# K^T V of two more batches in one float32 pass instead of three float16 passes, with a new issue order

## The chip, the cores and the metric

The kernel runs on one core of a Trainium2 chip. The metric is the device time of one execution in microseconds (us). The kernel before was timed at 987.38 us, the median of three runs (986.22 to 987.43 us).

## The reference, cut to what matters

Three layers are chained: a linear attention with exponential features, a gated feed-forward layer and an ELU feed-forward layer. All inputs are float32.

```python
# attention: B=4 batches, H=8 heads, S=576 tokens, D=64, m=128 features
phi(x) = exp(x @ omega.T - |x|^2/2 - max) / sqrt(m)     # per token and head: 128 features
q_p, k_p = phi(q / 64**.25), phi(k / 64**.25)
kv  = einsum('bhsm,bhsd->bhmd', k_p, v)                 # K^T V, one 128 x 64 matrix per batch and head
z   = sum(k_p, axis=2)
out = einsum('bhsm,bhmd->bhsd', q_p, kv) / (einsum('bhsm,bhm->bhs', q_p, z) + 1e-6)
# x: 2304 tokens x 512
xn  = rmsnorm(x) * rms_g
x   = (silu(xn @ w_gate) * (xn @ w_val)) @ w_out        # d_ff 1536
y   = elu(x @ w_in) @ w_out2                            # d_ff 2048
```

## The kernel before

Large products are made in float16 pairs: a float32 operand is split into a high part (rounded to float16) and a low part (the rest), and three products (high x high, high x low, low x high) are summed in PSUM. These products, with 256 columns each, make up the two feed-forward layers; the kernel calls them the spine. Nine blocks of 256 tokens go through them; the last layer uses a Strassen form with seven products.

The attention is cut into jobs. A *k job* takes one tile of 128 tokens of K (the fifth tile of a batch has 64), makes the features of 8 heads in `phi`, and adds this tile's part of K^T V to two PSUM banks, `acc`. A batch has five k jobs, so four batches have 20. A *q job* makes the features of 128 query tokens, multiplies them by the finished K^T V, divides, normalizes, and transposes the result for the spine. The k jobs of batches 0 and 1 run in the first 130 us, while weights are still loaded and split. Those of batches 2 and 3 lie between spine products; their tiles of K^T V run on TensorE at 293 to 326 us (batch 2) and 418 to 443 us (batch 3).

There are two ways to form K^T V, chosen by the batch number against `KV32` (2 in this kernel), in `k_job`, `values`, `phi` and `turned`:

- Batches below `KV32`: the features stay float32 (`phi` is called with `pair=False` and returns `d`). V is loaded as float32 with a column of ones for z (65 columns per head) from the input `v1`. Each head takes one float32 matmul, with V as the 65 weight columns and the features as 128 moving columns. The sum is K^T V transposed, 65 x 512 in each bank. After the last tile, `turned` splits it into a high and a low part (ScalarE and VectorE), turns each head back with a small float16 matmul against the identity (16 per batch: two parts of eight heads), and copies the results to the pair `kv_r` that the q jobs read.
- Other batches: V and the features are both split into float16 pairs. Per tile that is a copy to float16 and a subtraction over 1024 columns for the features (`halves` in `phi`) and a scaled copy and a subtraction over 512 columns for V (`values`). Each head takes three float16 matmuls with the features as 128 weight columns and 65, 64 and 65 moving columns. The last tile's sum is already in the right shape and is split once.

```python
e = phi(load, n, key, b >= KV32)
...
if b < KV32:
    pe.matmul(out=acc[h // 4][0:65, ...], lhsT=V32[:n, t, h], rhs=e[:n, h * P:(h + 1) * P], ...)
...
    pe.matmul(out=o, lhsT=kh, rhs=V[:n, t, h, 0:65], ...)
    pe.matmul(out=o[:, 0:64], lhsT=kh, rhs=V[:n, t, h, 65:129], ...)
    pe.matmul(out=o, lhsT=kl, rhs=V[:n, t, h, 0:65], ...)
```

The order of all work is set by a planner (`Plan`). Every operation is first recorded; then `deadlines` gives each a due time counted back from the spine, `order` plays the program through with estimated costs and takes on each engine the ready operation that is due first, and `play` issues the instructions in that order. All instructions therefore carry the line of `play` (L530) in the profile. The numbers that steer it (`BIAS` per job, `PRICE` for the choice between engines that can do the same step, `LOOK`, `INFL`, `LEAD`, `STRETCH`, `AHEAD`, `PELEAD`, and `BLIM` for PSUM banks held by the attention) stand at the head of the file. Names in the profile: RX, RW, RA, RM, RC, RS, RI and RO are areas of SBUF that are used for different things in turn, `ps` is any of the eight PSUM banks.

Of the kernel before, what the change touches and what calls it, by code (L numbers as in the profile page):

```python
# [22 lines left out]
NACT, SPLIT = '12111011102010110100001022111212110111', '00000000000000001111111111111111111111'  # L23
SPINE = [(0, 0), (0, 1), (0, 2), (1, 0), (1, 1), (0, 3), (0, 4), (1, 2), (0, 5), (1, 3), (1, 4), (1, 5)]
TPE = 1
KV32 = 2
HALF = 2
AHEAD, BLIM = 1540580.623, 6
QPE = 3
FINE = 9  # L30
BIAS = [1, -22, 0, -12, 8, 10, 1, -7, -6, 14, 26, 7, 0, 2, -36, -40, 59, 0, 26, -23, 0, -36, 41, -65, -115, 60, 0, -2, -73, -72, 0, -47, -43, -15, 226, -101, -257, -27, 0, 11, -9, -26, 15, 25, 55, 0, 3, 53, -60, 1, -17, 1, 102, 7, 7, -1, 0, 28, -17, 3, 56, 56]
LOOK, WEIGH = 0.076, 80
PRICE = [2.561, 1.313, 0.814, 2.417, 0.6, 0.917]
PELEAD = 127543.557
INFL, LEAD = 1.668, 51.224
STRETCH = (11.923, 880.565, 0.234)
NBLK = NT // NB
EXPM = 0x7F800000
SGN = -(1 << 31)
# [100 lines left out]
class Plan:  # L140
# [164 lines left out]
    def deadlines(self):  # L305
        at = 0.0
        for op in self.ops:
            op.due = 1e9
            if op.spine:
                op.due = at  # L310
                at += op.cost * (STRETCH[0] if at < STRETCH[1] else STRETCH[2])
        for op in reversed(self.ops):
# [3 lines left out]
    def order(self, limit=None):  # L316
        for op in self.ops:
            op.due -= BIAS[op.job] * (not op.spine)
        left = [len(op.deps) for op in self.ops]
# [74 lines left out]

        early, late = [dict(zip(("DVE", "ACT", "POOL"), p)) for p in (PRICE[:3], PRICE[3:])]
        idle = {kind: [x for x in xs if not x.closed] for kind, xs in self.slots.items()}
# [8 lines left out]
        while True:  # L405
# [37 lines left out]
            now, e = t, e = best  # L443
            op = min((op for op in queue[e] if op.now <= t + LOOK), key=lambda op: (op.due - (PELEAD if e == "PE" and not op.spine else 0.0), op.n))
            op.at = op.now
# [94 lines left out]
def fused(ctx: ExitStack, tc: tile.TileContext, qT, kT, kTt, qn, kn, v, v1, omT, eye, g, wg, wv, wo, w1, w2, out):  # L540
# [433 lines left out]
    def values(b):  # L974

        vraw = []
        for t in range(5):
            n = P if t < 4 else 64
            if b < KV32:
                sp.dma_start(out=V32[:n, t].rearrange("p h d -> p (h d)"), in_=v1[b * S + t * P:b * S + t * P + n])  # L980
            else:
# [3 lines left out]
                sp.dma_start(out=vraw[t], in_=v[b * S + t * P:b * S + t * P + n])  # L985
        if b < KV32:
            W = V32.rearrange("p t h d -> p (t h) d")[:, :, 0:64]
# [5 lines left out]
        vec.tensor_scalar(out=ivs[:, b:b + 1], in0=iv, scalar1=32768.0, scalar2=None, op0=ALU.mult)  # L993
        if b < KV32:
            vec.memset(sv, 2.0 ** -8)
# [30 lines left out]
    def k_job(b, t, key):  # L1026
# [9 lines left out]

        e = phi(load, n, key, b >= KV32)
        if t == 0:
            values(b)
        first, last = t == 0, t == 4  # L1040
        if first:
            acc[:] = [bank.next(), bank.next()]
        if b < KV32:
            with plan.group():
# [400 lines left out]
```

## Time and profile before

| | us |
|---|---|
| median of three runs | 987.38 |
| the profiled execution's own time | 987.1 |
| span from its first to its last instruction | 985.3 |
| TensorE (PE) busy | 919.1 |
| VectorE (DVE) busy | 662.1 |
| GpSimd (POOL) busy | 621.6 |
| ScalarE (ACT) busy | 541.7 |

The span is what the trace covers; 1.8 us lie around it. Busy time is the union of an engine's instructions. The clock that TensorE was granted was 0.972 of full speed on average; it is below full speed mainly in the first 130 us.

### The profile page before, as it was taken

How to read it: one execution, taken by the hardware profiler on the slowest of the kernel's cores; microseconds unless marked ns; L12 is line 12 of the kernel's file. 1: busy time of each engine (PE TensorE's matmuls, PEld its weight loads, DVE VectorE, ACT ScalarE, POOL GpSimd, SP SyncE). 2: the span in 40 equal slices, each digit the busy share in tenths (PEclk: the TensorE clock that was granted, in tenths of full speed). 3: DMA queues.
4: the chain of work that ended last, by engine and by line, in shares of the span. 5: the costliest groups of instructions: out<-in, count | busy, mean ns of one | idle time of the engine just before them, and what ended most of it. 6: DMA issues, size and time to landing. Idle time of an engine off the chain costs nothing. (4 is left out here: it accounts for less than half of the span.)

```text
span 985.3 us, 22369 instructions
## 1 busy us (share of the span) xinstructions
PE 919.1 (93%) x8904; PEld 808.2 (82%) x8904; DVE 662.1 (67%) x1618; ACT 541.7 (55%) x1014; POOL 621.6 (63%) x676
## 2 busy tenths in 40 slices
PE   6486789999989999999999999999999999999998
PEld 5386678788878878888887778888888888888887
DVE  6876899856678775768985886377626475365642
ACT  6886554625556756664643456777535564354630
POOL 2669766856969688788664568999515264152630
PEclk9587899999999999999999999999999999999999
DMA  9954554123331252124765433100000000000001
GB/s 260 231 155 142 161 173 169 28 55 87 76 87 55 66 108 71 33 77 140 187 220 130 137 120 108 65 1 7 12 23 12 12 12 17 18 17 12 12 12 43
DMA packets 82567, 82.57 MB, mean 84 GB/s; under 512 B 52896, under 2 KB 57888, under 8 KB 82464
## 3 DMA queue, kind: packets, MB, share of 16 engines
q1 hardware_dynamic: 82464, 81.16, 29.6%
q8 instruction: 69, 1.13, 0.5%
q14 instruction: 34, 0.28, 0.1%
HBM read 59.90 MB, written 8.91 MB: 70 GB/s over the span
## 5 line engine op out<-in xcount | busy, mean ns | idle before, releaser
L530 PEld LDWEIGHTS <-RW 128*128 128x128 f16 x4864 | 457.7, 99 | 79.3 <-issue 16.4
L530 PE MATMUL ps<-RM,RW 128*128 128x256 f16 (+1 forms) x3240 | 369.1, 272 | 5.7 <-POOL RW L530 2.4
L530 PEld LDWEIGHTS <-RA 128*128 128x128 f16 (+2 forms) x2984 | 257.6, 98 | 33.5 <-issue 3.6
L530 PE MATMUL ps<-RX,RA 128*128 128x256 f16 x1728 | 196.3, 273 | 1.3 <-DVE RM L530 1.2
L530 POOL TENSOR_TENSOR RA<-RA 64x512 f16<-64x512 f32 (+4 forms) x108 | 144.9, 1343 | 40.0 <-ACT RA L530 14.5
L530 ACT ACTIVATE RM<-ps,RC 128x512 f32<-128x512 f32 (+1 forms) x135 | 90.0, 669 | 103.1 <-PE ps L530 66.4
L530 ACT ACTIVATE RM<-RM 128x512 f32<-128x512 f32 (+3 forms) x166 | 98.1, 594 | 39.2 <-DVE RM L530 34.3
L530 DVE SCALAR_TENSOR_TENSOR ps<-ps,RM 128x512 f32<-128x512 f32 x72 | 50.2, 697 | 91.7 <-POOL RM L530 91.6
L530 POOL TENSOR_SCALAR RM<-RM,RC 128x512 f32<-128x512 f32 x72 | 55.3, 768 | 84.9 <-ACT RM L530 84.4
L530 POOL TENSOR_TENSOR RM<-RM 128x512 f16<-128x512 f32 (+1 forms) x97 | 95.7, 994 | 12.5 <-ACT RM L530 6.6
L530 DVE TENSOR_REDUCE RS<-ps 128x4 f32<-128x512 f32 (+5 forms) x146 | 75.0, 536 | 36.4 <-PE ps L530 36.0
L530 PE MATMUL ps<-RX,RW 128*128 128x256 f16 x864 | 98.5, 273 | 0.2 <-DVE RA L530 0.2
L530 ACT ACTIVATE RA<-RA 128x512 f32<-128x512 f32 (+3 forms) x88 | 66.7, 769 | 56.3 <-DVE RA L530 19.9
L530 DVE SCALAR_TENSOR_TENSOR RM<-RM,ps 128x512 f32<-128x512 f32 x108 | 73.0, 680 | 36.2 <-ACT RM L530 25.0
L530 POOL TENSOR_TENSOR RW<-RM,RW 128x256 f16<-128x256 f32 (+1 forms) x67 | 48.1, 727 | 39.3 <-ACT RW L530 24.8
L530 PE MATMUL ps<-RW 128*128 128x256 f16 x600 | 71.7, 273 | 0.9 <-DVE RM L530 0.9
L530 ACT ACTIVATE RA<-RA,RS 64x512 f16<-64x512 f32 (+3 forms) x71 | 53.0, 758 | 29.9 <-POOL RS L530 19.5
L530 PE MATMUL ps<-RW,RA 128*128 128x256 f16 (+2 forms) x560 | 67.0, 273 | 1.2 <-DVE RM L530 1.2
L530 POOL TENSOR_SCALAR RA<-RA,RS 64x512 f32<-64x512 f32 (+3 forms) x67 | 48.3, 721 | 24.9 <-ACT RA L530 21.4
L530 DVE TENSOR_TENSOR RM<-ps,RM 128x256 f32<-128x256 f32 x108 | 45.0, 420 | 10.5 <-ACT RM L530 6.2
L530 POOL TENSOR_SCALAR RX<-RX 128x512 int32<-128x512 uint32 x36 | 26.7, 742 | 40.1 <-DMA RX<-wg 13.9
L530 DVE SCALAR_TENSOR_TENSOR RM<-ps,RC,RM 128x256 f32<-128x256 f32 x54 | 25.1, 478 | 39.6 <-PE ps L530 35.7
(143 smaller groups left out, 1194.7 us busy)
## 6 DMA issues: line engine op xcount, KB each, us to landing
RA<-w SPq DMA_DIRECT2D x32, 512.0 KB, 4.0
RX<-wg SPq DMA_DIRECT2D x12, 512.0 KB, 5.2
RX<-wv SPq DMA_DIRECT2D x12, 512.0 KB, 6.0
RX<-wo SPq DMA_DIRECT2D x12, 512.0 KB, 4.9
out<-RM SPq DMA_DIRECT2D x36, 128.0 KB, 1.7
f<-RA SPq DMA_DIRECT2D x8, 512.0 KB, 3.0
RA<-f SPq DMA_DIRECT2D x8, 512.0 KB, 3.3
RA<-qn SPq DMA_DIRECT2D x11, 256.0 KB, 3.0
```

The lines of the kernel that those rows point to most:

```text
L530: getattr(real, fn)(*[fix(x) for x in a], **{i: fix(x) for i, x in k.items()})
```

## The change

`KV32` goes from 2 to 4, so all four batches take the float32 way. For the ten k jobs of batches 2 and 3 (eight tiles of 128 tokens, two of 64) the pairs of V and of the features are no longer made, and the 24 float16 matmuls per tile are replaced by 8 float32 matmuls. The host passes all of V with its column of ones. `turned` now runs for batches 2 and 3 too. The planner's numbers are other ones, and so the order on every engine is another. The table of `BIAS` has 62 numbers, of which most differ; its rows are left out here.

```diff
-KV32 = 2
+KV32 = 4
 HALF = 2
-AHEAD, BLIM = 1540580.623, 6
+AHEAD, BLIM = 3299112.986, 7
...
-LOOK, WEIGH = 0.076, 80
-PRICE = [2.561, 1.313, 0.814, 2.417, 0.6, 0.917]
-PELEAD = 127543.557
-INFL, LEAD = 1.668, 51.224
-STRETCH = (11.923, 880.565, 0.234)
+LOOK, WEIGH = 0.188, 80
+PRICE = [2.546, 1.318, 0.828, 2.103, 0.651, 0.872]
+PELEAD = 553133.854
+INFL, LEAD = 1.882, 50.766
+STRETCH = (9.752, 1069.521, 0.403)
```

Two places on TensorE's queue show what moved. The first is a tile of batch 2 in the middle of the program, among spine products (`ps<-RM,RW 128x256`). Before, LDWEIGHTS are the features and the rows with 64 columns are the products with the low part of V:

```order
L530 MATMUL ps_65<-RM,RW 128x256
L530 LDWEIGHTS RA
L530 MATMUL ps_62<-RA 128x65
L530 LDWEIGHTS RA
L530 MATMUL ps_62<-RA 128x64
L530 LDWEIGHTS RA
L530 MATMUL ps_62<-RA 128x65
```

Now three tiles of batch 2 follow each other there, each as two rows of four float32 matmuls (their weight loads are part of the row); RX and RA hold features and V:

```order
L530 LDWEIGHTS RW
L530 MATMUL ps_66<-RM,RW 128x256
L530 MATMUL ps_63<-RA 65x128 x4
L530 MATMUL ps_64<-RA 65x128 x4
L530 MATMUL ps_63<-RX,RA 65x128 x4
L530 MATMUL ps_64<-RX,RA 65x128 x4
L530 MATMUL ps_63<-RA 65x128 x4
L530 MATMUL ps_64<-RA 65x128 x4
L530 LDWEIGHTS RA
L530 MATMUL ps_68<-RA 128x65
```

In place of 24 short matmuls with their own weight loads a tile has 8 float32 ones, and the tiles are taken together.

The second place is the start of the spine on TensorE. Before, the first spine product (`ps_65<-RM,RW 128x128`) follows a q job's last product and three small matmuls that spread a maximum (RI, RS):

```order
L530 MATMUL ps_61<-RA,RW 128x65
L530 LDWEIGHTS RS
L530 MATMUL ps_62<-RI,RS 1x128
L530 LDWEIGHTS RI
L530 MATMUL ps_62<-RS,RI 128x1
L530 LDWEIGHTS RS
L530 MATMUL ps_64<-RI,RS 1x128
L530 LDWEIGHTS RW
L530 MATMUL ps_65<-RM,RW 128x128
```

Now two float32 tiles of batch 1 and the projection of another k job (`<-RC,RA 128x128`, eight rows) stand ahead of the first spine product, which comes 12 rows further on:

```order
L530 MATMUL ps_64<-RI,RM 128x128
L530 MATMUL ps_68<-RA 65x128 x4
L530 MATMUL ps_62<-RA 65x128 x4
L530 MATMUL ps_67<-RC,RA 128x128
L530 MATMUL ps_61<-RC,RA 128x128
```

Before, these two tiles stood behind the first 24 rows of the spine.

## Rows read from the trace of the kernel before

**Rows 1.** The page: busy time, share of the span and instructions of TensorE
```profile
PE 919.1 (93%) x8904; PEld 808.2 (82%) x8904; DVE 662.1 (67%) x1618; ACT 541.7 (55%) x1014; POOL 621.6 (63%) x676
```

**Rows 2.** Windows: length, busy time of five engines, TensorE's clock, DMA share
```profile
0.00:150.00 150.00, 106.47 (x976) 95.14 (x977) 117.36 (x303) 101.00 (x180) 98.31 (x112) 0.84 0.67 187
150.00:600.00 450.00, 435.11 (x4492) 377.59 (x4492) 337.65 (x816) 242.68 (x405) 323.91 (x306) 0.99 0.39 104
600.00:985.00 385.00, 377.48 (x3439) 335.49 (x3437) 207.06 (x500) 198.06 (x430) 199.43 (x259) 1.00 0.06 20
...
200.00:300.00 100.00, 96.61 (x1000) 83.40 (x998) 64.17 (x177) 48.61 (x76) 70.62 (x72) 0.98 0.34 78
300.00:400.00 100.00, 98.04 (x1055) 85.69 (x1053) 71.82 (x184) 62.01 (x113) 83.08 (x83) 0.98 0.32 76
```

**Rows 3.** Waits of TensorE from 200 to 500 us: total, times, longest
```profile
PE ps L530 <- DVE RS L530: 2.4, 3, 1.1
PE ps L530 <- DMA RM<-RA: 2.0, 1, 2.0
PE ps L530 <- POOL RA L530: 0.9, 1, 0.9
```

**Rows 4.** Waits of TensorE from 500 to 640 us
```profile
PE ps L530 <- DVE RA L530: 3.7, 4, 2.2
PE ps L530 <- DVE RS L530: 3.3, 4, 1.3
```

**Rows 5.** Waits of TensorE from 150 to 200 us, the longest in total
```profile
PE ps L530 <- POOL RW L530: 2.4, 3, 1.2
```

**Rows 6.** Timeline of TensorE (start, length): two tiles of batch 2, what follows
```profile
292.94 0.90 PE L530 MATMUL ps<-RA 128*128 128x65 f16 x24
293.68 0.90 PE L530 MATMUL ps<-RA,RX 128*128 128x65 f16 x24
294.42 1.06 PE L530 MATMUL ps<-RO,RA 128*128 128x128 f16 x16
```

**Rows 7.** Groups by form on TensorE: rows with 64 columns, float16 k tiles alone
```profile
L530 PE MATMUL ps<-RA 128*128 128x64 f16 x40 | 4.0, 195 | 0.0
L530 PE MATMUL ps<-RA,RX 128*128 128x64 f16 x24 | 2.5, 195 | 0.0
L530 PE MATMUL ps<-RA,RX 64*128 64x64 f16 x16 | 1.7, 192 | 0.0
```

**Rows 8.** Timeline of TensorE: four float32 tiles of batch 0 in a row
```profile
58.02 7.29 PE L530 MATMUL ps<-RW,RA 128*65 128x128 f32 x64
65.25 0.22 PE L530 MATMUL ps<-RI,RS 128*2 128x128 f16 x1
```

**Rows 9.** Timeline of TensorE: a quarter of turned for batch 1
```profile
132.00 0.29 PE L530 MATMUL ps<-RI,RA 65*128 65x65 f16 x4
132.12 1.48 PE L530 MATMUL ps<-RM,RW 128*128 128x256 f16 x12
```

**Rows 10.** Groups by form on ACT, POOL, DVE: pairs of features, steps of turned
```profile
L530 ACT ACTIVATE RA<-RA 128x1024 f16<-128x1024 f32 x13 | 13.8, 1060 | 2.1 <-POOL RA L530 1.3
L530 POOL TENSOR_TENSOR RA<-RA 128x1024 f16<-128x1024 f32 x18 | 38.4, 2132 | 19.8 <-ACT RA L530 14.5 <-DVE RS L530 3.1 <-DVE RC L530 1.6
L530 ACT ACTIVATE RA<-ps,RC 65x512 f16<-65x512 f32 x2 | 1.2, 676 | 0.0
L530 DVE SCALAR_TENSOR_TENSOR RA<-ps,RC,RA 65x512 f16<-65x512 f32 x2 | 1.4, 730 | 0.0
```

**Rows 11.** Waits of TensorE from 0 to 150 us, the two longest in total
```profile
PE ps L530 <- DVE RS L530: 16.0, 7, 4.5
PE ps L530 <- ACT RW L530: 10.9, 7, 5.1
```

**Rows 12.** Groups by form of weight loads: float16 features, float32 V
```profile
L530 PEld LDWEIGHTS <-RA 128*128 128x128 f16 x2888 | 254.0, 98 | 32.6 <-issue 2.8 <-POOL RA L530 2.2 <-DVE RM L530 1.0
L530 PEld LDWEIGHTS ps<-RW,RA 128*65 128x65 f32 x64 | 7.0, 138 | 0.1
```

More of the change, by code (lines that the diff above doesn't have):

```diff
@@ L25 @@
 TPE = 1
-KV32 = 2
+KV32 = 4
 HALF = 2
-AHEAD, BLIM = 1540580.623, 6
+AHEAD, BLIM = 3299112.986, 7
 QPE = 3
 FINE = 9
-BIAS = [1, -22, 0, -12, 8, 10, 1, -7, -6, 14, 26, 7, 0, 2, -36, -40, 59, 0, 26, -23, 0, -36, 41, -65, -115, 60, 0, -2, -73, -72, 0, -47, -43, -15, 226, -101, -257, -27, 0, 11, -9, -26, 15, 25, 55, 0, 3, 53, -60, 1, -17, 1, 102, 7, 7, -1, 0, 28, -17, 3, 56, 56]
-LOOK, WEIGH = 0.076, 80
-PRICE = [2.561, 1.313, 0.814, 2.417, 0.6, 0.917]
-PELEAD = 127543.557
-INFL, LEAD = 1.668, 51.224
-STRETCH = (11.923, 880.565, 0.234)
+BIAS = [1, -23, -4, -4, 8, 10, 6, -6, -8, 20, 28, 4, 6, -1, -28, -78, 104, 0, -43, -37, -5, -37, 38, -145, -110, -3, -4, -9, -29, -44, -7, 0, -33, 48, 123, -93, -395, -46, 0, 13, -13, -40, -1, 224, 51, -14, -1, 134, -12, 74, -14, 12, 281, 20, 0, -3, 10, 47, -17, 3, 1, 0]
+LOOK, WEIGH = 0.188, 80
[3 more added lines that the diff above has]
+STRETCH = (9.752, 1069.521, 0.403)
 NBLK = NT // NB
```

## The prediction

> **What bounds the kernel now.** I read the busy shares first: TensorE is busy for 919.1 of 985.3 us, and no other engine is above 67% [rows 1]. A busy share is an average, so the windows come next. From 150 us on TensorE is nearly without gaps: it is idle for 450.0 - 435.1 = 14.9 us between 150 and 600 us and for 385.0 - 377.5 = 7.5 us after that, but for 150.0 - 106.5 = 43.5 us in the first 150 us, where VectorE, ScalarE and GpSimd prepare weights and features [rows 2]. So there are two regimes. Work added to TensorE at the start may be hidden in its waits, while work added after 150 us moves the end one for one unless a wait disappears for it. The third view is the waits of TensorE by stage. Between 200 and 500 us they come to 5.3 us in three groups, 2.4 us of it on VectorE, 2.0 us on a transposing DMA and only 0.9 us on GpSimd [rows 3]. Between 500 and 640 us it waits 7.0 us, all on VectorE [rows 4].
>
> The edit belongs to the second regime. The K^T V tiles of batches 2 and 3 run at 293 to 443 us. The order after keeps them there: three tiles of batch 2 follow each other among spine products, as the first pair of pieces shows.
>
> **The change part by part.**
>
> *Float16 tiles removed.* The products with 64 columns exist in these tiles alone, and there are 40 + 24 + 16 = 80 of them, eight per tile: ten tiles [rows 7]. Two tiles that follow each other start 0.74 us apart, and the next group starts 0.74 us after that [rows 6]; I count starts because the last matmul's end overlaps what follows. Ten tiles take 7.4 us. That the two tiles with 64 tokens cost the same is taken over from the full ones: the moving columns are the same.
>
> *Float32 tiles added.* The same step exists for batch 0: four tiles in a row take 65.25 - 58.02 = 7.23 us, or 1.81 us each [rows 8]. They have 8 heads with 128 moving columns, exactly what the new tiles have. Ten take 18.1 us. Net: 18.1 - 7.4 = +10.7 us on TensorE.
>
> *turned added.* A quarter of it delays the spine by 132.12 - 132.00 = 0.12 us [rows 9]; four quarters and two batches are +1.0 us. It also brings a chain that was not there: ScalarE (676 ns) and VectorE (730 ns) split each of two banks, TensorE turns, and two engines copy out [rows 10], before the first q job of that batch can multiply. TensorE has spine products to run meanwhile: in the new order four quarters of batch 2 stand apart from each other with spine rows between them. I cost the latency at nothing. Without that cover it would be two banks in a row, 2 x (0.68 + 0.73) = 2.8 us per batch, 5.6 us in all.
>
> *Pairs no longer made.* Each of ten tiles loses a copy to float16 (1.06 us on ScalarE where it goes there) and a subtraction (2.13 us on GpSimd) [rows 10], so up to 10.6 us of ScalarE and 21.3 us of GpSimd go, and more for V. These engines are busy for 242.7 and 323.9 of 450 us in that stage [rows 2], so they do not set the end; the saving is worth only those waits of TensorE that it removes. Lowest is nothing. Highest is all of TensorE's idle time from 150 to 600 us, 14.9 us, plus the time that a lowered clock cost: the granted clock is 0.98 in each of the windows 200 to 300 and 300 to 400 us [rows 2], which is 0.02 x 200 = 4.0 us. I take a value near the low end, 0.9 us, the wait on GpSimd that stands in the stage itself [rows 3]. The waits on VectorE I leave where they are, because VectorE is given turned's steps and loses little, and those after 500 us come from splitting the weights of the last layer, which the change does not touch.
>
> *New order.* At the start two float32 tiles of batch 1 and a projection now stand ahead of the first spine product, as the second pair of pieces shows. The projection is 8 float32 matmuls of 128 columns as well, so three times 1.81 us, 5.4 us of TensorE time, moved forward. TensorE waits there anyway, 16.0 us for VectorE's small reductions and 10.9 us for ScalarE [rows 11], so I cost it at nothing; uncovered it is +5.4 us. It could also help, as the tiles are then out of the way later, where TensorE is already dense: they take 3.6 us there. Between -3.6 and +5.4 us I take 0, the value that the wide idle time of the start is nearest to.
>
> *Sum.* The profiled execution took 987.1 us, of which the span is 985.3 us. 987.1 + 10.7 + 1.0 - 0.9 = 997.9 us. The median of the runs lies 0.3 us above the profiled execution, so 998.2; I forecast 998 us.
>
> [...] Loading 128 float16 columns of weights takes 98 ns and there are 24 loads in a tile, and yet the tile passes in 0.74 us [rows 6, 12]: the loads overlap each other or the matmuls. [...]
>
> **The rivals.**
>
> *First, the other side: TensorE's waits go.* Place: between spine products from 150 to 640 us. The jobs of batches 2 and 3 lose their pairs, features and weights are ready earlier, and TensorE finds its operands when it comes to them. Price: up to 14.9 + 4.0 = 18.9 us back against 11.7 us added, 987.1 + 11.7 - 18.9 = 979.9 us at the extreme. It decides from 13.7 us recovered (11.7 us plus 2 us of resolution), about three quarters of all that is there; its time is some 983 us. For it: GpSimd is busy for 72% of that stage and TensorE waits on it there and, for 2.4 us, between 150 and 200 us [rows 5]. Against it: most of the waits are on VectorE and on a DMA [rows 3, 4], and a new order brings waits of its own.
>
> *Second: the start becomes longer.* The three groups moved ahead of the spine are not hidden, because what they need from ScalarE and VectorE is on the same path as the first spine products: +5.4 us, 1003.6 us with the median's 0.3 us. For it: TensorE's waits at the start are on these two engines [rows 11]. Against it: 43.5 us of idle time [rows 2].
>
> *Third: weight loads set the pace of small matmuls.* Then a float16 tile costs 24 x 98 ns = 2.35 us and a float32 one 16 x 138 ns = 2.21 us [rows 12]; ten tiles and turned are -1.4 + 1.0 = -0.4 us, 987 us. Against it stands the direct spacing of 0.74 us [rows 6].
>
> That the change does not do what it says is ruled out by the order: the rows with 64 columns are gone and ten pairs of float32 rows have come.
>
> **How the numbers follow.** The forecast has a chance of 0.76; its own range is 993 to 1004 us (the lower bound with 5 us of waits recovered, the upper with turned's latency open). The longer start has 0.08, the waits that go 0.13, and weight loads that set the pace 0.03. A difference of 0.2%, 2 us, is about what a measurement of this kernel can tell from no change. Slower by more than that are the longer start and the forecast but for a tail of 0.05 in which recovered waits eat the addition nearly up: 0.08 + 0.71 = 0.79. Within it: 0.05 + 0.03 = 0.08. Faster: 0.13. The range that holds the time 8 times in 10 is 985 to 1005 us: it reaches past the third rival at 987 and past the second at 1003.6, and leaves out most of the first.
>
> **What the profile of the changed kernel would show.** Right: float32 groups of 65 weight columns with twice the count, 1.8 us per tile at 290 to 450 us; TensorE's busy time up by 11 to 12 us, to about 931 us; its idle time about as before, some 66 us; GpSimd and ScalarE less busy. The spine's stages from 640 us on keep their length and start some 10 us later. Wrong: TensorE idle for less than 53 us in all would mean that the waits paid for the work. A first spine product more than 3 us later than before, with the end later by as much beyond the 11 us, would be the second rival. Float32 tiles that take 2.8 us would mean a lowered clock where they run, 10 us more. Less than 0.5 us between the old and the new tile would mean that I took the cost of a tile wrongly.

## The result and the profile after

The changed kernel took 992.81 us, the median of 5 runs (992.01 to 996.73), beside 987.38 us of the kernel before (986.22 to 987.55): a ratio of 1.0072, 95% interval 1.0047 to 1.0097. In a later set of runs (a1 below) it took 993.89 us, the median of 12 runs, beside 990.1 us: 1.0036 (1.0017 to 1.0056). It is slower by about 4 to 5.5 us. 998 us was forecast, 10.6 us more than before: the sign was right, the size two to three times too large. The profiled execution took 996.55 us, 3.7 us above its own median, with a span of 994.8 us.

The busy line answers to [rows 1]:

```profile
PE 930.3 (94%) x8856; PEld 818.6 (82%) x8856; DVE 657.7 (66%) x1636; ACT 524.3 (53%) x989; POOL 568.1 (57%) x635
```

TensorE has 11.2 us more work and GpSimd 53.5 us less. TensorE's idle time is 994.8 - 930.3 = 64.5 us, 1.7 us less than before. In a1's profile (span 992.1 us, TensorE busy 930.6 us) it is 61.5 us.

The windows (length, busy time of PE, PEld, DVE, ACT, POOL, clock, DMA share, GB/s) answer to [rows 2]:

```profile
0.00:150.00 150.00, 105.57 (x970) 94.94 (x971) 119.87 (x305) 99.72 (x179) 97.40 (x110) 0.86 0.70 199
150.00:600.00 450.00, 439.05 (x4381) 381.80 (x4381) 323.77 (x808) 222.38 (x379) 266.86 (x263) 0.99 0.37 99
```

The middle stage became denser, but this one row hides that two things of opposite sign happened in it. Finer windows of the kernel before show where it was idle:

```profile
150.00:200.00 50.00, 46.62 (x460) 40.46 (x460) 45.04 (x83) 25.93 (x39) 37.62 (x29) 1.00 0.29 88
200.00:500.00 300.00, 294.48 (x3183) 257.14 (x3180) 215.55 (x543) 171.24 (x299) 227.69 (x225) 0.99 0.36 91
500.00:640.00 140.00, 133.03 (x1208) 114.09 (x1206) 94.08 (x228) 73.66 (x115) 98.43 (x90) 1.00 0.42 126
```

The same windows of the changed kernel:

```profile
150.00:200.00 50.00, 44.51 (x416) 37.63 (x416) 39.36 (x88) 27.14 (x41) 33.20 (x27) 0.93 0.25 69
200.00:500.00 300.00, 299.09 (x3091) 263.62 (x3089) 206.85 (x530) 152.31 (x271) 191.74 (x193) 1.00 0.35 88
500.00:640.00 140.00, 135.18 (x1239) 115.51 (x1237) 96.92 (x243) 71.07 (x113) 79.57 (x79) 1.00 0.40 127
```

Length minus TensorE's busy time gives its idle time by stage, in us (the last line is the total less the others):

| stage | before | after | after, a1 |
|---|---|---|---|
| 0 to 150 | 43.5 | 44.4 | 42.7 |
| 150 to 200 | 3.4 | 5.5 | 5.5 |
| 200 to 500 | 5.5 | 0.9 | 0.5 |
| 500 to 640 | 7.0 | 4.8 | 4.8 |
| from 640 | 6.8 | 8.9 | 8.0 |
| total | 66.2 | 64.5 | 61.5 |

From 200 to 640 us the waits fell by 6.8 us; from 150 to 200 us they grew by 2.1 us and the clock fell from 1.00 to 0.93 there.

The waits of TensorE (who it waited for, us in total, times, longest) from 200 to 500 us answer to [rows 3]; its three groups are gone (a fourth of 0.2 us, not shown there, makes the 5.5 us of the table), and this one has come:

```profile
PE ps L530 <- DMA RX<-RA: 0.7, 1, 0.7
```

From 500 to 640 us, answering to [rows 4]:

```profile
PE ps L530 <- DVE RA L530: 2.1, 4, 0.9
PE ps L530 <- DVE RS L530: 1.7, 4, 0.6
PE ps L530 <- DMA RX<-RA: 0.6, 1, 0.6
```

From 150 to 200 us, answering to [rows 5]; the waits on GpSimd are gone, and one of 4.0 us on VectorE has come:

```profile
PE ps L530 <- DVE RW L530: 4.0, 1, 4.0
PE ps L530 <- DVE RC L530: 1.5, 1, 1.5
```

The timeline of TensorE (start, length) shows the first new tiles of batch 2 and a quarter of turned, answering to [rows 6, 8, 9]:

```profile
295.92 1.91 PE L530 MATMUL ps<-RA 128*65 128x128 f32 x16
297.67 1.91 PE L530 MATMUL ps<-RX,RA 128*65 128x128 f32 x16
299.41 2.65 PE L530 MATMUL ps<-RA 128*65 128x128 f32 x40
...
328.40 0.29 PE L530 MATMUL ps<-RI,RX 65*128 65x65 f16 x4
328.52 1.48 PE L530 MATMUL ps<-RM,RW 128*128 128x256 f16 x12
```

The first new tile takes 297.67 - 295.92 = 1.75 us where 1.81 us were predicted, and this quarter of turned 0.12 us as predicted. From start to start the ten new tiles take 1.75 to 1.89 us, 18.2 us in all; the ten old ones took 0.74 to 0.84 us, 7.8 us in all; the eight quarters take 0.12 to 0.22 us, 1.3 us in all.

Counting the 7032 spine products of 256 columns by their order in the trace, the start of the n-th (us) shows when time is lost and regained:

| n | before | after | a1 |
|---|---|---|---|
| 0 | 104.5 | 102.7 | 102.0 |
| 200 | 154.7 | 155.2 | 153.8 |
| 300 | 165.6 | 168.6 | 167.2 |
| 400 | 178.0 | 186.8 | 185.3 |
| 2000 | 397.3 | 398.5 | 397.0 |
| 2300 | 437.2 | 447.2 | 445.8 |
| 4000 | 645.8 | 653.3 | 650.6 |
| last | 981.8 | 990.9 | 988.3 |

The spine starts 1.8 us earlier and loses that and 0.5 us more by n = 200. It loses 8.3 us from there to n = 400, between 155 and 187 us, long before the first new tile. It regains 7.6 us by n = 2000 although batch 2's tiles lie in that stretch, and loses 8.8 us again where all five tiles of batch 3 are.

**What happens at 160 to 175 us.** TensorE in the changed kernel (the bracket is the idle time ahead of a row and who ended it):

```profile
164.63 5.41 PE L530 MATMUL ps<-RM,RW 128*128 128x256 f16 x48
174.07 0.27 PE L530 MATMUL ps<-RI,RC 128*6 128x128 f16 x1 [4.03 <-DVE RW L530]
174.28 6.76 PE L530 MATMUL ps<-RM,RW 128*128 128x256 f16 x36
```

VectorE meanwhile:

```profile
161.42 1.21 DVE L530 TENSOR_REDUCE RS<-RA 128x1 f32<-128x1024 f32 x1
...
163.14 0.67 DVE L530 TENSOR_REDUCE RS<-RA 64x1 f32<-64x512 f32 x1
...
168.55 0.47 DVE L530 TENSOR_SCALAR RX<-RX 128x512 uint16<-128x512 uint16 x1
172.25 0.43 DVE L530 TENSOR_SCALAR RW<-RX 128x512 int32<-128x512 int32 x1 [3.23 <-DMA RX<-wo]
```

And SyncE's queue, which issues the loads, in the changed kernel and then in the kernel before:

```profile
152.63 13.24 SPq L530 DMA_DIRECT2D RX<-wo  x4
```

```profile
146.46 15.16 SPq L530 DMA_DIRECT2D RX<-wo  x7
```

The first two rows of VectorE are two of the three pieces of the maximum of V for batch 2, which the new order places here (the first piece stands at 106.63 us; before, five shorter pieces stood between 149.61 and 195.27 us). Then VectorE stands for 3.23 us at an instruction that needs the last part of w_out. That load is the last of four issued between 152.63 and 165.87 us; before, the last was issued by 161.62 us and VectorE did not wait for it. The queue waits for VectorE to free RX, as the waits of SyncE's queue from 140 to 170 us show:

```profile
SPq L530 <- DVE RX L530: 18.7, 3, 10.1
```

Before, the queue waited for VectorE too (12.3 us for RX, 10.2 and 7.9 us for two other areas), so this wait alone does not tell why the load is later now. What VectorE owes the spine is queued behind the waiting instruction, and TensorE waits 4.03 us. Behind that gap the 36 spine products take 6.76 us, 188 ns each, against 5.41 / 48 = 113 ns ahead of it: 36 x 75 = 2.7 us more, at a granted clock of 0.66 from 170 to 180 us. Before, the same 36 took 4.10 us. VectorE ran nothing else in its 3.23 us of waiting: one row ends at 168.55 + 0.47 = 169.02 us, the next starts at 172.25 us.

### The profile page after: what moved, and what is told of

It is laid out like the page before. It is cut to its first block, busy times and chain, and to the rows that moved or that the text cites. A ratio compares the mean times of both kernels' runs of the same rounds, so it can differ in the third digit from the quotient of the medians.

```text
span 994.8 us, 22202 instructions
## 1 busy us (share of the span) xinstructions
PE 930.3 (94%) x8856; PEld 818.6 (82%) x8856; DVE 657.7 (66%) x1636; ACT 524.3 (53%) x989; POOL 568.1 (57%) x635
## 5 line engine op out<-in xcount | busy, mean ns | idle before, releaser
L530 PEld LDWEIGHTS <-RA 128*128 128x128 f16 (+1 forms) x2928 | 256.2, 98 | 34.1 <-issue 3.0
L530 PE MATMUL ps<-RX,RA 128*128 128x256 f16 (+2 forms) x1776 | 201.9, 273 | 1.2 <-DVE RM L530 1.2
L530 POOL TENSOR_TENSOR RA<-RA 64x512 f16<-64x512 f32 (+4 forms) x93 | 116.7, 1255 | 45.1 <-DVE RS L530 12.5
L530 ACT ACTIVATE RM<-RM 128x512 f32<-128x512 f32 (+3 forms) x159 | 93.9, 594 | 46.0 <-DVE RM L530 39.3
L530 DVE TENSOR_REDUCE RS<-ps 128x4 f32<-128x512 f32 (+4 forms) x146 | 75.5, 536 | 34.3 <-PE ps L530 32.4
L530 ACT ACTIVATE RA<-RA 128x512 f32<-128x512 f32 (+4 forms) x82 | 61.3, 758 | 57.2 <-DVE RA L530 20.9
L530 ACT ACTIVATE RA<-RA,RS 64x512 f16<-64x512 f32 (+3 forms) x64 | 48.3, 757 | 46.6 <-DVE RS L530 15.8
L530 POOL TENSOR_TENSOR RW<-RM,RW 128x256 f16<-128x256 f32 (+1 forms) x65 | 45.4, 710 | 36.3 <-ACT RW L530 24.7
L530 POOL TENSOR_TENSOR RA<-RM,RA 128x256 f16<-128x256 f32 x48 | 31.7, 671 | 31.0 <-ACT RA L530 22.5
```

What stands on the lines that cost most here:

```text
L530: getattr(real, fn)(*[fix(x) for x in a], **{i: fix(x) for i, x in k.items()})
```

## The experiments

Each keeps all else of the kernel that it starts from. "Spine product 400" is the start of the 400th in the trace.

**The changed kernel again, unaltered** (a1), in a later set of runs.

> The changed kernel unaltered, for a second profile. Its five times fell into two groups, 992.0 to 992.8 and 996.6 to 996.7 us, and the profile on record is of the upper one (span 994.8 us, TensorE busy 930.3 us, idle 64.5 us). If the two groups differ in how long TensorE waits at the start (5.5 us of waits between 150 and 200 us in the first profile, and the spine 7 to 9 us late there), a profile of the lower group (span about 991 us) has TensorE busy for 930 us again and about 4 us less idle time before 200 us. If they differ in the granted clock, the mean clock is higher and the busy time lower by 4 us, with the idle time the same.

Measured: 993.89 us (990.31 to 997.53, 12 runs) beside 990.1 us (986.9 to 993.97): 1.0036 (1.0017 to 1.0056). Its columns in the tables above show the same pattern: TensorE's work up by 11.5 us, waits from 200 to 500 us nearly gone, the loss at n = 400 there. What differs from the first profile is the first 150 us (1.7 us less idle time, where 4 were expected before 200 us) and later small waits; the busy time is the same. The changed kernel takes nearly the same time in both sets (992.8 and 993.9 us); the kernel before differs more (987.4 and 990.1 us).

**The change taken apart** (b1, c0, c1). With the new numbers of the planner and the old way of summing:

```diff
 # the changed kernel
-KV32 = 4
+KV32 = 2
```

> KV32 back to 2, with the new planner's numbers: the new numbers alone. Theory 1 (TensorE has 11 us more to do and the new numbers' order gives 5 to 6 us back by itself): about 981 to 982 us, TensorE busy about 919 us, waits between 200 and 500 us about 1 us as in the changed kernel. Theory 2 (the order is worth nothing by itself; the jobs without pairs relieve GpSimd and ScalarE, and this removes the waits): 987 us or more, waits between 200 and 500 us of 5 us or more again. The numbers were not chosen for this value of KV32, which can make it slower than either says.

Measured: 1038.06 us, ratio 1.049 (1.0454 to 1.0526). And the float32 sums alone, under the old numbers with one PSUM bank less for the attention, beside the old way with the same numbers:

```diff
 # the kernel before; c0: this line alone, c1: KV32 = 4 as well
-AHEAD, BLIM = 1540580.623, 6
+AHEAD, BLIM = 1540580.623, 5
```

> The kernel before with BLIM 5 in place of 6 (with 6, the old numbers give no complete order for KV32 = 4); a base for the next run. Both theories: near 987 us, with a few us either way, as it is another order.

> The kernel before with BLIM 5 and KV32 = 4: the float32 way alone, with the old numbers, to be set against the run with BLIM 5 and KV32 = 2. Theory 1 (11 us more on TensorE, nothing comes back by itself): 11 to 12 us slower than that run, TensorE busy 11 us more, idle time the same. Theory 2 (relief of GpSimd and ScalarE gives 5 to 6 us back): 5 to 6 us slower, TensorE's idle time 5 to 6 us less, the difference between 200 and 500 us.

Measured: c0 1045.2 us (1.0556, 1.0528 to 1.0585), c1 1067.19 us (1.0779, 1.0745 to 1.0812). b1's expectation had allowed for a slower order; c0 and c1 missed plainly. The window of 150 to 640 us tells why, first b1, then c0:

```profile
150.00:640.00 490.00, 444.44 (x4468) 382.12 (x4467) 329.30 (x825) 247.39 (x413) 320.92 (x303) 0.94 0.36 97
```

```profile
150.00:640.00 490.00, 434.29 (x4362) 375.38 (x4361) 336.58 (x790) 233.11 (x390) 314.93 (x295) 0.93 0.34 91
```

TensorE is idle for 46 and 56 us there and its clock is at 0.94 and 0.93. The planner's numbers fit one set of operations; with another set, or one number changed, the order falls apart by 48 and 55 us, some ten times the effect in question. The change can't be split in this way. Between the profiled executions of c0 and c1 lie 17.8 us: TensorE's busy time is 15.6 us higher, 4 us more than tiles and turned cost, and its idle time 2.2 us higher. So under the old numbers no wait paid for the tiles, but these are orders with over 100 us of idle time.

**The tiles' price by itself** (d1). The new tiles are multiplied twice, in the order of the changed kernel. The sums and z both double, so their quotient stays.

```diff
+                plan.open.twice = 2 if b >= 2 else 1   # issue this group's matmuls twice
                 for h in range(8):
```

> The changed kernel and its order, with the float32 K^T V matmuls of batches 2 and 3 issued twice (the sums of numerator and denominator both double), so ten tiles more on TensorE. Theory 1 (TensorE is the bound there and a tile costs 1.81 us, one for one): 18 us slower, TensorE busy 18 us more. Theory 2 (the tiles lie partly in time that TensorE would wait): less than 13 us slower, with less idle time.

Measured: 1012.14 us (1008.41 to 1014.39), ratio 1.0253 (1.0226 to 1.028). Two doubled tiles on TensorE, and the busy line:

```profile
295.53 3.66 PE L533 MATMUL ps<-RA 128*65 128x128 f32 x32
299.02 3.66 PE L533 MATMUL ps<-RX,RA 128*65 128x128 f32 x32
```

```profile
PE 950.8 (94%) x9016; PEld 839.2 (83%) x9016; DVE 656.3 (65%) x1636; ACT 525.2 (52%) x989; POOL 569.0 (56%) x635
```

A doubled tile takes 3.49 us, twice 1.75; the last spine product starts 17.1 us later, for ten tiles of 1.75 = 17.5 us. 18 us were expected, and by the ratios it is 18 to 21 us more than the changed kernel. Added work in this stage moved the end one for one. (TensorE's busy time rose by 20.5 us; 3.5 us of that lie in the first 150 us, at a clock of 0.84 beside 0.86.)

**GpSimd's load put back** (g1). In the changed kernel the subtractions of 1024 columns that GpSimd makes in q jobs are issued twice. They are fourteen, not eleven as was expected, and GpSimd has 31.6 us more.

```diff
             halves(d[:n, c], e[:n, 0, c], e[:n, 1, c])
+            plan.ops[-1].again = key >= FINE   # GpSimd issues it twice
```

> The changed kernel and its order, with GpSimd's subtraction for the features' low part issued twice in the q jobs (11 times 2.1 us, 23 us more on GpSimd between 175 and 450 us, about what the change took from it); the second writes the same values again. Theory 1 (TensorE's waits between 200 and 500 us, 5.3 us before and 0.7 us after, went because GpSimd was relieved): they come back, 4 to 5 us of waits and some lowered clock, 4 to 8 us slower. Theory 2 (they went with the new order): waits between 200 and 500 us stay under 1.5 us and the time within 1.5 us of the changed kernel.

Measured: 1005.08 us (999.8 to 1007.31), ratio 1.0176 (1.0149 to 1.0203). By the ratios that is 10 to 14 us more than the changed kernel, where 4 to 8 were expected. TensorE's waits from 200 to 500 us:

```profile
PE ps L530 <- DVE RS L530: 2.0, 3, 0.7
PE ps L530 <- DVE RA L530: 1.6, 2, 1.2
PE ps L530 <- POOL RA L530: 1.1, 2, 0.6
PE ps L530 <- DMA RX<-RA: 0.7, 1, 0.7
PE ps L530 <- DMA RM<-RA: 0.3, 1, 0.3
```

They are 5.7 us, where the changed kernel has 0.7 and the kernel before 5.5. From 500 to 640 us they are 7.1 us, and the clock falls again at 360 to 380 us (0.95 and 0.88) and at 510 to 530 us (0.96 and 0.87). TensorE's idle time from 200 to 640 us is 13.0 us, 7.3 more than in the changed kernel, and the clock costs, as an estimate from these four windows, 10 x (0.05 + 0.12 + 0.04 + 0.13) = 3.4 us. Most of the returned wait is not on GpSimd but on VectorE behind it. So the new order needs the room that the pairs left on GpSimd. One weakness: each doubled step also lengthens the chain of its q job by 2.1 us, so load and latency are not separated.

**The relief alone, in the old order** (i1, j1). In the kernel before, the low part of the k features of batches 2 and 3 is not subtracted on GpSimd: in i1 it is filled with zero on VectorE, which leaves the low part out of the sums; in j1 VectorE makes the subtraction.

```diff
+            plan.ops[-1].klo = kjob   # i1: memset on VectorE; j1: the subtraction on VectorE
```

> The kernel before and its order, with GpSimd's subtraction for the features' low part in the ten k jobs of batches 2 and 3 (2.1 us each) replaced by a fill with zeros on VectorE; the low part of these features is left out of the result, TensorE's work is as before. Theory 1 (relief of GpSimd is what removed TensorE's waits between 200 and 500 us): these fall from 5.3 us to under 2 us in the old order too, and the time by 5 to 9 us, to 979 to 982 us beside 987. Theory 2 (the new order removed them): the waits stay at 4 us or more and the time within 2 us.

> The kernel before and its order, with these ten subtractions given to VectorE in place of GpSimd, full and exact (at 1.1 to 1.2 us each about 12 us more for VectorE, 21 us less for GpSimd). Theory 1 (GpSimd's load is what counts): 3 to 7 us faster, 980 to 984 us, which would beat both kernels. Rival (VectorE is what TensorE waits for, 2.4 us in 200 to 500 us and 7.0 us after it): no change or slower, waits on VectorE up by 3 us or more.

Measured: i1 991.11 us, ratio 0.9995 (0.9975 to 1.0015); j1 992.21 us, 1.001 (0.999 to 1.003), beside 990.82 us. GpSimd is relieved by 20.1 us in i1, and TensorE's waits from 200 to 500 us are these:

```profile
PE ps L533 <- DVE RS L533: 2.4, 3, 1.0
PE ps L533 <- DMA RM<-RA: 2.0, 1, 2.0
PE ps L533 <- POOL RA L533: 0.8, 1, 0.8
PE ps L533 <- POOL RW L533: 0.2, 1, 0.2
```

The groups of [rows 3] stand there nearly unaltered, and j1 has 2.4, 2.0, 0.8 and 0.6 us. VectorE's busy time rose by 7.0 us in j1, from 662.1 to 669.1 us, where about 12 were expected. Both gains forecast for a relieved GpSimd failed to come. In the old order this relief buys nothing. It is 20.1 of the 53.5 us that the change takes from GpSimd, and ScalarE is not relieved; the whole relief in the old order was not run.

**The wait at 170 us: who has to come later?** (f1, f2, h1, k1). First, the two small products that spread w_out's scales, at which TensorE stands, are issued 36 spine products later each (f1), and those of the last layer's first weights 24 and 12 later too (f2):

```diff
+HOLD = lambda job, n: (3, 3) if n == 6 else (0, 0)                       # f1
+HOLD = lambda job, n: (3, 3) if n == 6 else (2, 1) if job == 57 else (0, 0)   # f2
```

> The changed kernel, and its order, with one step moved: the two small matmuls that spread the scales of w_out (RI,RC 6x128 and RI 128x6), for which TensorE waited 4.0 us at 170 us, stand 36 and another 36 spine matmuls further back in TensorE's queue; on VectorE what needs them moves with them. Theory 1 (the start of the changed kernel lost some 6 us because TensorE stood in its queue behind a matmul whose data came late, with spine work ready behind it): the wait and the lowered clock after it go, 4 to 5 us faster than the changed kernel, about 988 to 989 us in a set of runs where that takes 993 to 994 us. Theory 2 (w_out's scaling is late itself and the spine needs it): the 4 us come back as a wait at the first products with w_out, and the time stays.

> As the run with w_out's spread moved, and for the splits of the last layer's first weights too (500 to 640 us) each first spread matmul 24 and each second one another 12 spine matmuls further back. Theory 1: TensorE's waits between 500 and 640 us (4.4 us in the changed kernel, 7.0 before) fall under 1 us, and the time by another 3 to 4 us, to about 985 us. Theory 2 (VectorE is late with the splits, so that the waits only move): no more than 1 us beside the run with w_out's spread alone.

Measured: f1 995.24 us, 1.0086 (1.0059 to 1.0113); f2 996.89 us, 1.0101 (1.0077 to 1.0125), beside 987.42 us. The wait of f1 at the same place:

```profile
PE ps L531 <- DVE RM L531: 4.5, 1, 4.5
```

Spine product 400 starts at 187.3 us, not earlier, and the forecast of 988 to 989 us failed. TensorE no longer waits for the scales but for RM, the spine's own next step on VectorE, which stands behind the same late load (3.11 us). In f2 the waits from 500 to 640 us became one group of 4.9 us: moved as well, not under 1 us.

Then the maximum of V of batch 2 is held back on VectorE by 168 spine products (h1):

```diff
-    ma = largest([W[:, 0:16], W[:, 16:32], W[0:64, 32:40]])
+    ma = largest([W[:, 0:16], W[:, 16:32], W[0:64, 32:40]], b == 2)   # hold = 14
```

> The changed kernel and its order, with one chain moved: VectorE's reductions for the largest |V| of batch 2 (1.2, 1.2 and 0.7 us at 161 to 164 us, ahead of the step that frees a buffer for the last part of w_out) wait until 168 more spine matmuls have been issued. Theory 1 (the start is late because VectorE makes this chain first, the last load of w_out starts after it, and VectorE then stands 3.2 us in its queue for that load): the 3.2 us and TensorE's 4.0 and 1.5 us of waits at 164 to 174 us mostly go, and spine matmul 400, at 185 to 187 us in the changed kernel, comes at 182 to 183 us; 3 to 5 us faster in the end. Theory 2 (the load is late for another reason, as the queue it stands in): spine matmul 400 stays at 185 us or later.

Measured: 991.13 us (988.85 to 994.3, 12 runs) beside 990.82 us (29 runs), ratio 1.001 (0.9987 to 1.0034). Spine product 300 starts at 163.3 us, 400 at 181.2, the last at 986.1. TensorE's waits from 150 to 200 us:

```profile
PE ps L530 <- DVE RW L530: 3.9, 1, 3.9
PE ps L530 <- DVE RC L530: 0.7, 1, 0.7
```

The wait of 4 us, which should have gone, is as long as ever; everything around it came 4 to 5 us earlier, and w_out's loads are issued from 148.49 us on instead of 152.63. Most of this lead is there before the two reductions at 161 us could matter: spine product 200 starts at 150.8 us already, against 155.2 us (a1: 153.8). The hold also moves the first piece of the maximum, from 106.63 to 128.20 us, and TensorE hardly waits at turned of batch 1 (that this piece is the reason is not shown). The changed kernel has four waits there, 3.6 us in all, of which these are two, and a clock of 0.83 from 140 to 150 us:

```profile
142.47 0.29 PE L530 MATMUL ps<-RI,RA 65*128 65x65 f16 x4 [1.72 <-ACT RA L530]
...
145.20 2.35 PE L530 MATMUL ps<-RM,RW 128*128 128x256 f16 x12 [0.82 <-ACT RA L530]
```

In h1 the first two quarters pass at once, only one wait of 0.57 us is left, and the clock is 1.00:

```profile
141.05 0.63 PE L530 MATMUL ps<-RI,RA 65*128 65x65 f16 x8
```

From spine product 200 to 400 h1 takes 30.4 us, the changed kernel 31.6 (a1: 31.5), the kernel before 23.3. So the two reductions are worth about 1 us of the 8.3 us lost there, and why the load comes later than before is not shown. The ratios of a1 and h1 differ by 0.26%, but their intervals overlap; the gain rests on the trace more than on the times.

Last, h1 and f1 together, with VectorE's step for the late part of w_out held back by 60 spine products (k1):

```diff
+                plan.ops[-1].hold = 5 if plan.job == 49 and i == 1 else 0
```

> As h1, and in addition what VectorE does for the last part of w_out's words (it waits for a load that comes late) is held back 60 spine products, and the two small products that spread w_out's scales 36 each, so that VectorE makes the spine's next step first and does not stand behind the load. Theory 1 (the 3.9 us of waiting that h1 still has near 168 us are a head-of-line stop of VectorE behind that load): the wait goes, the 400th spine product starts 3 to 4 us earlier than in h1 (about 177 to 178 us), and the end comes 2 to 4 us earlier than h1's, 987 to 989 us, ratio to the kernel before 0.996 to 0.999. Theory 2 (the spine itself needs the load or what depends on it by then): a wait of about the same size appears somewhat later, the 400th spine product stays at 180 to 182 us, and the time is that of h1, ratio 1.000 to 1.003.

Measured: 996.66 us (994.67 to 998.82), beside 987.13 us: 1.0096 (1.0072 to 1.012). TensorE:

```profile
160.97 13.27 PE L530 MATMUL ps<-RM,RW 128*128 128x256 f16 x120
179.73 0.27 PE L530 MATMUL ps<-RI,RS 128*1 128x128 f16 x1 [5.48 <-DVE RS L530]
```

The stop at the load is gone (120 products in a row), and 5.48 us of waiting stand 11 us later, at the maximum of V, which VectorE reaches at 177.68 us only. This is the second theory, and worse than it said. VectorE is 8.01 and 8.00 us busy in the windows from 160 to 170 and 170 to 180 us, which leaves little room: what was put off here was missed a little later. No version of the changed kernel here beats the kernel before.

## Why the prediction was right in sign and too large

*Tiles and turned: right.* +11.7 us were forecast, TensorE's busy time rose by 11.2 and 11.5 us, and the rows give 18.2 - 7.8 + 1.3 = 11.7 us. GpSimd and ScalarE became less busy by 53.5 and 17.4 us, as said. That work here moves the end one for one is shown by d1 (17.1 us for 17.5).

*Pairs no longer made, "0.9 us": the term that was mis-sized.* The waits from 200 to 640 us fell by 12.5 - 5.7 = 6.8 us, and the stretches of lowered clock went. These are the windows of before, then the only one of after from 150 to 660 us:

```profile
280.00:290.00 10.00, 6.76 (x61) 5.11 (x62) 6.84 (x23) 4.60 (x6) 8.05 (x7) 0.83 0.34 80
340.00:350.00 10.00, 8.04 (x89) 6.60 (x87) 6.80 (x26) 5.46 (x13) 9.31 (x11) 0.96 0.43 79
350.00:360.00 10.00, 10.00 (x100) 8.44 (x98) 7.66 (x22) 6.66 (x12) 7.50 (x9) 0.87 0.70 134
```

```profile
170.00:180.00 10.00, 5.97 (x30) 4.18 (x30) 6.76 (x16) 4.15 (x8) 3.62 (x4) 0.66 0.23 57
```

As an estimate from the clocks of these windows, 10 x (0.17 + 0.04 + 0.13) = 3.4 us at full clock were lost before. Together 10.2 us, between the bounds of 0 and 18.9. The reason given for the low end was that most of these waits are on VectorE and on a DMA, which the change does not relieve. For the old order i1 and j1 show it, as far as they relieve GpSimd. But the order was new too: with room on GpSimd it left hardly any of them from 200 to 500 us and 4.8 of 7.0 us after that, and g1, which takes the room away, has them back. The step read the waits of the old order as a property of the work.

*New order, "0 us": wrong on the other side.* From 150 to 200 us 2.1 us of idle time were added and 2.7 us of clock lost (the 36 slow products), 4.8 us, near the bound of +5.4. It was not the three groups moved ahead on TensorE: the first spine product starts 1.8 us earlier than before. It was VectorE standing at w_out's late load, a place that the prediction did not look at. The forecast's place of danger (TensorE's queue) was the wrong one. The maximum of V is about 1 us of it by h1; what makes the load late stays open.

*The sum with these sizes:* 987.1 + 11.7 - 10.2 + 4.8 = 993.4 us. The table has two more terms, 0.9 us of waits in the first 150 us and 2.1 us from 640 us on, which gives 996.4 us against 996.55 us of the profiled execution that all these terms are from. The same sum for a1 (its waits from 200 to 640 us are 5.3 us, the first 150 us give 0.8 us back, and the waits from 640 us add 1.2 us) is 993.4 us, against 993.93 us of its profiled execution. The errors had opposite signs and left 4 to 5 us: that the total of idle time stayed "about as before", as forecast, was luck. The forecast's own range began at 993 us, with 5 us of waits recovered; the first median lies at its edge because 10.2 us were.

*The rivals.* The first (waits go, and the kernel is faster) was half there: 10.2 us recovered of the 13.7 us from which it decides, and the start took 4.8 us back. The second has a longer start, but by another mechanism. The third is out: TensorE's busy time rose by 11.2 us, and a new tile takes 1.75 to 1.89 us where an old one took 0.74 to 0.84.

*What stays open:* how much of the 10.2 us is due to the planner's numbers alone, as b1, c0 and c1 could not separate it; why w_out's last load comes later in the new order; and why the profiled execution of the first set lies 3.7 us above its median. The spans of the two profiles differ by 2.7 us, half of it by n = 300.

## What to carry to other kernels

Waits in a profile belong to an order of issue: when the change brings a new order, bound what it recovers by all the waits of the stage, not by those on the relieved engine, and read the new order on VectorE and on the queue of the loads as closely as on TensorE. An instruction on VectorE that waited 3.23 us for a late load delayed what TensorE needed behind it (TensorE waited 4.03 us), and putting off VectorE's other work moved the wait instead of removing it (4.5 us in f1, 5.48 us in k1). When an edit moves a step, compare the traces from the first place that it touched: h1's lead was mostly won ahead of the place that it was aimed at. This planner's numbers could not be kept while the work changed: taking the change apart cost about 50 us where 5 were in question.

## What the runs showed of the hardware

Some gaps of TensorE cost more than their length here. In the kernel before, waits of 0.97, 0.37 and 2.05 us within 4 us were followed by 12 spine products in 1.99 us and 24 in 3.84 us, at a granted clock of 0.83 from 280 to 290 us; a little later 24 take 2.79 us:

```profile
281.41 0.16 PE L530 MATMUL ps<-RS,RI 1*128 1x1 bf16 x1 [0.37 <-DVE RS L530]
283.62 1.99 PE L530 MATMUL ps<-RM,RW 128*128 128x256 f16 x12 [2.05 <-DMA RM<-RA]
285.65 3.84 PE L530 MATMUL ps<-RM,RW 128*128 128x256 f16 x24
...
290.31 2.79 PE L530 MATMUL ps<-RM,RW 128*128 128x256 f16 x24
```

The wait of 4.03 us in the changed kernel was followed by 2.7 us of the same kind, 6.7 us in all. Not every gap does this: 1.46 us ending at 164.40 us in the changed kernel were followed by 48 products in 5.41 us, 113 ns each.
